# Dilated attention beside a state-space scan: the first weight columns loaded in another cut, and the order of every engine written anew

## The chip, the core and the metric

The kernel runs on one core of one Trainium2 chip. The time is device microseconds of one execution, from start to end. One execution was also recorded by the hardware profiler; its span, its rows and its chain of waits are what this document reads. Engine names are those of the profile: PE is TensorE's matmul side and PEld its weight loads, DVE is VectorE, ACT is ScalarE, POOL is GpSimd, SP is SyncE, whose sequencer here only issues DMAs.

## The reference, cut to what matters

Two independent layers work on inputs of their own, and their outputs stand side by side. A is attention with 16 heads of 28 channels over 2048 tokens, in which a token sees itself and seven earlier ones, two apart. B is a diagonal complex recurrence over the 2048 tokens with a projection in and out.

```python
S, D, H, Dh, W, dil = 2048, 448, 16, 28, 8, 2
# A
q, k, v = split_heads(x @ wqkv)                       # (H, S, Dh) each
logits = einsum("hsd,hswd->hsw", q, k[:, s - 2*w]) * Dh**-0.5   # -1e9 where s - 2w < 0
o = einsum("hsw,hswd->hsd", softmax(logits), v[:, s - 2*w])
a = merge_heads(o) @ wo
# B
Lam_bar = exp(exp(log_dt) * Lam)                      # 448 complex values
Bu = x @ (((Lam_bar - 1) / Lam)[:, None] * Bmat).T
for t in range(S): h = Lam_bar * h + Bu[t]; hs[t] = h
b = 2 * real(hs @ Cmat.T) + x * Dskip
out = concatenate([a, b], axis=-1)                    # (1, 2048, 896) bf16
```

## The kernel before

**The order is a string.** Each small function of the kernel is a step: it emits one group of instructions. `ORDER` names the steps one after the other, and the loop at the end calls them so. No scheduler moves anything afterwards, so every engine runs its own instructions in the order of the string, and an instruction that waits holds up everything behind it on its engine. In a name the digits are the arguments, `@` gives the PSUM banks that the step's matmuls write, and the last sign of an eviction (a copy out of PSUM) says which engine makes it: `.` is ACT, `=` is DVE; evictions without a sign that add something (`h`, `c`, `dn`) are DVE's.

**Attention's projections.** The 2048 tokens are two halves of 1024 (`u`), each of two blocks of 512 (`s`). The channels of q and k are cut into seven blocks `m`: 0, 2, 4 are 128 columns of q each, 1, 3, 5 the same of k, and 6 holds the last 64 of both, copied together by POOL (line 223). The contraction of 448 is three slices of 128 rows and one of 64; the slice of 64 rows is kept twice (partitions 0 to 63 and 64 to 127, `w_half`), so that the two token blocks run side by side on the two halves of the array. `QK u m 0` is the six matmuls of 128 rows, `QK u m 1` the two of 64, `QS m s` does one token block alone, `V_` is the same for v. `qk`, `qh`, `v` evict.

x must first be transposed. For tokens 0 to 1023 PE does it: `XI0`, `XI1`, `XI2` for tokens 0 to 511, `XH1`, `XA10`, `XA11` for tokens 512 to 1023, evicted by `xi`, `xh`, `xa`. For tokens 1024 to 2047 four DMA transposes do it (line 173).

**Logits and softmax.** `P u r w` (line 379) multiplies a block of q with four shifted views of k on DVE, 128 x 2048 elements into one of seven buffers; `E_ u r` sums such products over the channels of a head on PE. `lt`, `TD` (a DMA transpose), `sma`, `smb`, `smc` make the softmax of a half. `AL g` and `al` place its weights for four token tiles, `ad`, `sp` (four DMAs each) write them through DRAM into a banded matrix `PT`; `AX`, `ax`, `adx`, `spx` do the same for the seam between the halves. `AV B hg par` multiplies the band with v, `av` evicts into `oT`, `W_` applies `wo`, `w` evicts into one of six buffers `ya`, and `ow` stores.

**The recurrence.** `ty`, `tf`, `ts` make tables of sines (ACT and DVE), `BU` projects, `BR`, `z`, `UP`, `y` combine four tokens, `sa`, `sb`, `sd` scan on DVE, `DN`, `dn`, `H_`, `h` spread the states again, `ca` (two ACT instructions) and `cs` scale the output weights, `C` and `c` project and add, `oc` stores. The last product is cut in two (`CH`, `ch`, `oh`). `pg` is a row of 17 small DVE instructions, `rb` builds four rotation matrices.

**Loads.** All DMA of data is issued by SP but the first four, which ACT issues. Eight semaphores are used in turn, so that a DMA waits until the eighth before it has landed. `w_load(c, n, at)` loads `n` columns from `c` for 384 rows, one DMA for each offset in `at` (0 is q, D is k, 2D is v); `w_half(s, c, n, at)` loads the last 64 rows into half `s`.

Of the kernel before, what the change touches and what calls it, by code (L numbers as in the profile page):

```python
# [14 lines left out]
S, D, H, DH, W = 2048, 448, 16, 28, 8  # L15
# [14 lines left out]


ORDER = """
WU@0 XI0@0 xi00= xi01. XI1@1 XI2@2 xi10= xi11. PP@3 xi20. pcopy pa QS00@4 pb QS10@5 qk000. pd_ pc XH1@6 pe XA10@7
xh1. XA11@1 qk010. xa10= QK021@32 xa11. QK031@04 P000 ty0 QS01@6 pf QS11@5 P001 QK051@71 QK030 tf0 qk011. qk001. pg
ts00 QK050 qk031. ts10 ts20 QK020 qk051. P010 qk050. ty5 V_010@56 ty2 tf5 qk020. QK061@41 P011 V_001@73 ts05 V_011
V_000 v010. qk030. tf2 ts15 QK060 qk021= ts25 v000. P020 v001. QK040@50 qh001. rb2 v011. qh011. QK041 V_111@27 ty1
P021 V_101@36 V_110 qk040. qk041. tf1 ts02 E_00@50 P030 E_01 ts01 ts12 E_02 qh000. V_100 P031 qh010. v111. P040
QK130@41 ts22 ts11 v101. P041 v100. V_411@76 ts21 QK131 E_03 hc0 P050 ty6 E_04 ty4 V_410 qk131. tf6 qk130. QK100@31
P051 v411. ts06 v410. P060 QK110@46 ts16 BD v110. ts26 P061 QK101 ty3 QK151@72 QK111 qk100. E_05 rb0 qk101. E_06
qk110. QK150 tf4 lt00 P100 V_401@31 qk151. V_501@45 V_500 rb3 qk150. xt1 ts04 P101 lt01 QK120@27 ts14 qk111. tf3  # L40
v501. QK140@06 xt0 v500. P110 ts03 QK121 P111 QK141 qk120. QK161@54 V_400 qk140. xt3 P120 ts13 qk121. QK160 v400.
P121 qk141. v401. E_10@20 xt2 ts23 P130 E_11 ts24 V_510@73 qh101. P131 qh110. qh111. E_12 TD0 qh100. P140 E_13 hc1
V_511 P141 v511. v510. LC BU301@61 BU201@45 P150 BU300 sma0 BU200 OZ z30. XR BU400@37 z20. P151 smb0 BU000@64 P160
BR31 P161 BU001 ci1. BU401 E_14 z00. E_15 ci2= CD1 z40. E_16 rb1 z31. BR21 BR01 lt11 BU500@63 ci0= CD2 z21. smc0
z01. BU211@10 ci3. CD0 BU311@54 BU501 BU310 lt10 z50. CD3 BR32 BR41 BU210 z41. xd3 TD1 z32. BR51 xd2 BR22 AL0@2 z51.
BR33 z22. BU100@67 al0= z33. xd0 ca3 ad0 BU011@53 BU111@12 BU101 sma1 OP pm3 BU010 z10. pm0 wo UP3 AL1@6 cs3 smb1
BR11 xd1 BR02 BU110 z02. smc1 z11. BR03 al1. BR12 BU510@57 z03. ad1 z12. pm1 sp0 ca6 UP0 BR13 BU600@61 z13. y3. y0.
cs6 UP1 BR23 BU601 y1. z23. BU511 sa0 BU411@43 z60. BR52 pm4 ca1 BU410 sp1 sb0 BR61 z52. BR42 BU611@26 ca2 BU610 pm2
sd0 z61. AX@5 z42. BR53 BR62 AL2@1 ax= z53. z62. cs1 DN0@4 UP5 adx UP2 al2. DN1@5 BR43 dn0 BR63 y2. dn1 AL3@2 ad2
z63. sa2 H_10@1 y5. H_20@4 z43. H_11@0 al3. UP6 UP4 H_21@5 y6. H_00@7 ad3 y4. H_01@2 AV011@6 ca4 h21 spx AV010@3 h20  # L50
AV030@5 h01 av011. sp2 AV000@4 av010. cs2 AV020@6 av030. sb2 AV021@2 av000. AV001@3 av020. AV031@5 sd2 av001. W_00@4
sp3 av031. av021. W_20@6 ca5 h11 DN2@3 W_01@5 h00 DN3@2 dn2 w20. W_10@0 dn3 w01. sa4 ow20 W_11@7 ow01 W_21@3 w11.
w10. H_03@6 h10 H_02@2 w00. H_22@5 cs4 W_30@7 w21. ow00 sb4 H_23@0 ow21 H_13@1 w30. W_31@4 ow10 ca0 ow30 h13 AV100@3
ow11 h03 AV110@7 sd4 AV111@1 av110. AV131@6 av111. AV101@7 h02 av131. AV121@1 sa6 av101. AV130@6 av121. AV120@2 cs0
av130. DN5@7 av100. cs5 W_71@1 av120. dn5 W_61@6 w31. sb6 w71. h23 H_05@3 ow31 W_51@2 w61. ow71 ow61 W_41@7 w51= h05
H_15@4 ow51 H_25@1 W_50@0 h15 sd6 DN4@6 W_60@2 w50. w41. W_40@3 ow50 w60= ow41 DN6@4 C32@0 w40. ow60 dn6 dn4 ow40
h25 H_06@7 H_16@2 H_04@3 h06 H_12@4 H_14@6 h04 W_70@1 c32 H_24@7 C31@3 h22 oc32 w70= h12 C33@0 ow70 c31 h14 oc31
H_26@5 C30@1 c33 h26 oc33 h24 C02@4 c30 oc30 C20@3 c02 C00@6 c20 h16 oc20 CH0@0 c00 C01@5 oc00 C11@7 c01 ch0 oc01
C12@1 oh0 oc02 C13@4 C22@3 C03@2 c22 c12 oc22 c13 C21@6 oc12 c11 oc13 oc11 C10@5 c21 c03 oc21 CH1@0 oc03 c10 ch1
oc10 oh1  # L60
"""

# [1 line left out]
def kernel(  # L64
# [18 lines left out]
    ACT = nc.scalar  # L83
# [41 lines left out]
    def w_load(c, n, *at):  # L125

        for d in at:
            SP.dma_start(wq[:, 0:3, c + d:c + d + n], wq_r[:, :, c + d:c + d + n])  # L128

    def w_half(s, c, n, *at, eng=SP):  # L130

        o, i = (bass.AP(t.tensor, t.offset + c + at[0], [list(t.ap[0]), [D, len(at)], [1, n]])
                for t in (wq[64 * s:64 * s + 64, 3], A_wqkv[384:448]))
        eng.dma_start(o, i)
# [2 lines left out]
    for i, vec in enumerate((B_Lambda_re, B_Lambda_im, B_log_dt)):  # L137
        ACT.dma_start(raw[:, i], vec.rearrange("(g p) -> g p", p=64).unsqueeze(1).to_broadcast((G, 2, 64)))

    w_half(0, 0, 128, 0, D, eng=ACT)  # L140
    SP.dma_start(xnA[:, 0:2], xA_r[:, 0:2])
    SP.dma_start(xnA[:, 2:4], xA_r[:, 2:4])
    w_load(0, 128, 0, D)
    SP.dma_start(xnA[:, 4:8], xA_r[:, 4:8])
    w_half(1, 0, 256, 0, D)
    w_load(128, 128, 0, D)
    w_half(0, 128, 128, 0, D)
    w_load(256, 192, 0, D)
# [771 lines left out]
```

## Time and profile before

| | us |
|---|---|
| median of 3 runs (lowest, highest) | 133.71 (133.06, 136.21) |
| the profiled execution, whole | 132.89 |
| its span, first to last recorded work | 130.7 |
| PE busy, 1067 matmuls | 125.4 (96%) |
| DVE busy | 113.4 (87%) |
| ACT busy | 88.8 (68%) |
| first matmul on data (`XI0`) | 3.73 |
| first matmul of a projection (`QS00`) | 5.50 |
| last group of matmuls (`CH1`) starts | 126.95 |

The granted TensorE clock is full over the whole page. A time with a step's name is the start of that step's instructions in the trace; times count from the start of the span. Busy time of PE counts from a matmul's start to its modelled end, and neighbours overlap, so the text goes by the distance between starts.

### The profile page before, as it was taken

How to read it: one execution, taken by the hardware profiler on the slowest of the kernel's cores; microseconds unless marked ns; L12 is line 12 of the kernel's file. 1: busy time of each engine (PE TensorE's matmuls, PEld its weight loads, DVE VectorE, ACT ScalarE, POOL GpSimd, SP SyncE). 2: the span in 40 equal slices, each digit the busy share in tenths (PEclk: the TensorE clock that was granted, in tenths of full speed). 3: DMA queues.
4: the chain of work that ended last, by engine and by line, in shares of the span. 5: the costliest groups of instructions: out<-in, count | busy, mean ns of one | idle time of the engine just before them, and what ended most of it. 6: DMA issues, size and time to landing. Idle time of an engine off the chain costs nothing.

```text
span 130.7 us, 2869 instructions
## 1 busy us (share of the span) xinstructions
PE 125.4 (96%) x1067; PEld 62.2 (48%) x1067; DVE 113.4 (87%) x206; ACT 88.8 (68%) x185; POOL 19.8 (15%) x37
## 2 busy tenths in 40 slices
PE   6999999999999999999999999999899999999991
PEld 6543443434233334334454356854575555565550
DVE  5679999999999999999999899999997999752282
ACT  1779999999978996995979999997497300000000
POOL 6802000000000000200799920000000000000000
PEclk9999999999999999999999999999999999999999
DMA  3997989899999998999786999999412332213043
GB/s 116 238 207 174 326 230 167 197 197 258 139 259 210 212 200 187 310 303 209 209 200 222 185 169 293 255 179 185 141 54 70 105 105 94 87 55 103 0 146 118
DMA packets 47780, 23.24 MB, mean 178 GB/s; under 512 B 35639, under 2 KB 46711, under 8 KB 47767
## 3 DMA queue, kind: packets, MB, share of 16 engines
q1 hardware_dynamic: 47560, 23.03, 78.3%
q8 instruction: 8, 0.13, 0.4%
q10 hardware_dynamic: 207, 0.04, 0.2%
q14 instruction: 5, 0.04, 0.1%
HBM read 11.69 MB, written 6.37 MB: 138 GB/s over the span
## 4 chain that ended last, share of the span: by engine, by line
PE 80%; ACT 7%; DMA 6%; SPq 3%; issue 1%; DVE 0%; ACTq 0%
PE ps L244 38%; PE ps L807 15%; PE ps L547 6%; PE ps L534 5%; PE ps L391 5%; ACT ctmp L684 4%; DMA out_dram<-ya 3%; PE ps L722 3%; DMA wq<-in_A_wqkv_dram 3%; PE ps L788 3%; ACT Z L114 2%; SPq L128 2%; PE ps L348 1%; PE ps L827 1%; PE ps L395 1%
## 5 line engine op out<-in xcount | busy, mean ns | idle before, releaser
L379 DVE TENSOR_TENSOR pr<-qf,kf 128x2048 bf16<-128x2048 bf16 x24 | 28.7, 1236 | 0.1
L244 PE MATMUL ps<-xbuf,BT 128*128 128x512 bf16 (+1 forms) x112 | 23.6, 380 | 0.0
L244 PE MATMUL ps<-xT,wq 128*128 128x512 bf16 (+1 forms) x96 | 20.6, 380 | 0.1
L807 PE MATMUL ps<-Cw,Z 128*128 128x448 bf16 x105 | 20.5, 352 | 0.0
L114 ACT CAST Z<-ps 128x512 bf16<-128x512 f32 (+1 forms) x35 | 15.8, 520 | 3.0 <-PE ps L722 1.5
L813 DVE TENSOR_TENSOR xbuf<-ps,xnB 128x448 bf16<-128x448 f32 x15 | 9.0, 620 | 7.6 <-PE ps L807 7.5
L244 PEld LDWEIGHTS <-BT 128*128 128x128 bf16 (+1 forms) x112 | 8.9, 97 | 12.6 <-issue 3.5
L807 PEld LDWEIGHTS <-Z 128*128 128x128 bf16 x105 | 10.3, 98 | 9.4
L793 DVE TENSOR_TENSOR Z<-ps,Z 128x512 bf16<-128x512 f32 x21 | 13.7, 680 | 0.2 <-PE ps L788 0.2
L547 PE MATMUL ps<-wo,oT 128*128 128x448 bf16 x64 | 13.6, 353 | 0.0
L244 PEld LDWEIGHTS <-wq 128*128 128x128 bf16 (+1 forms) x96 | 7.8, 97 | 11.0 <-issue 2.3
L244 PE MATMUL ps<-wq,xT 128*128 128x448 bf16 (+1 forms) x64 | 13.0, 354 | 0.0
L877 POOL MEMSET PT<- 128x4320 f32 x3 | 11.0, 3698 | 7.2 <-DVE xnB L797 7.2
L114 ACT CAST ya<-ps 128x448 bf16<-128x448 f32 (+1 forms) x14 | 7.0, 566 | 5.5 <-PE ps L547 2.8
L684 ACT ACTIVATE ctmp<-Cw,c2t 64x448 f32<-64x448 bf16 x14 | 9.3, 667 | 0.3
L547 PEld LDWEIGHTS <-oT 128*128 128x128 bf16 x64 | 6.2, 98 | 5.7 <-ACT oT L114 0.2
L534 PE MATMUL ps<-PT,v_s 128*32 128x135 bf16 (+1 forms) x256 | 8.8, 298 | 0.0
L114 ACT CAST oT<-ps 128x512 bf16<-128x512 f32 x17 | 8.7, 620 | 0.1
L244 PEld LDWEIGHTS <-xT 128*128 128x128 bf16 (+1 forms) x64 | 4.8, 97 | 7.5 <-issue 4.1
L114 ACT CAST v_s<-ps 128x448 bf16<-128x448 f32 x16 | 8.2, 542 | 0.1
L534 PEld LDWEIGHTS <-v_s 128*32 128x32 bf16 x256 | 7.0, 110 | 0.7 <-ACT Z L114 0.4
L114 ACT CAST kf<-ps 128x512 bf16<-128x512 f32 x12 | 6.7, 582 | 0.7 <-PE ps L244 0.7
(150 smaller groups left out, 180.9 us busy)
## 6 DMA issues: line engine op xcount, KB each, us to landing
PT<-pd SPq DMA_DIRECT2D x16, 156.0 KB, 5.2
xnB<-in_B_x_dram SPq DMA_DIRECT2D x2, 896.0 KB
out_dram<-ya SPq DMA_DIRECT2D x16, 112.0 KB, 1.7
out_dram<-xbuf SPq DMA_DIRECT2D x15, 112.0 KB, 1.7
pd<-Ak SPq DMA_DIRECT2D x2, 640.0 KB, 3.5
xbuf<-in_A_x_dram SPq DMA_DIRECT2D x2, 448.0 KB
xnB<-in_B_x_dram SPq DMA_DIRECT2D x4, 224.0 KB, 5.4
xnB<-in_B_x_dram SPq DMA_DIRECT2D x4, 192.0 KB, 4.0
```

What stands on the lines that cost most here:

```text
L114: (ACT.copy if e == "A" else V.tensor_copy)(o, i)
L244: PE.matmul(o, l, r, start=(first and i == 0), stop=(not first and i == len(pairs) - 1 and not more[s]))
L379: V.tensor_tensor(t[:], q.unsqueeze(1).to_broadcast((128, 4, 512)), k4, ALU.mult)
L391: PE.matmul(acc[s][32 * i:32 * i + 32], E[:, f, ws, :], t[:, i, :], start=(f == 0 and ws == 0), stop=False)
L534: PE.matmul(p[32 * hh:32 * hh + 32, 128 * bl:128 * bl + n], v_s[:, t, 4 * hg + hh, :], PT[:, t % NS, (4 * hg + hh) // HS, (4 * hg + hh) % ...
L547: PE.matmul(p[:, 0:D], late["oT"][:, b // 4, hg, par, 128 * (b % 4):128 * (b % 4) + 128], late["wo"][:, hg, :], start=(hg == 0), stop=(hg ...
L684: ACT.activation(t[a:a + 64, 0:D], Cw[b:b + 64, g, :], ACTF.Copy, scale=c2t[a:a + 64, g:g + 1])
L722: PE.matmul(pp["z", g, j][:], rot(g, 0), late["Z"][:, g, j - 1, :], start=False, stop=True)
L793: V.tensor_tensor(zz, pp.pop(("h", j, g))[:], zz, ALU.add)
L807: PE.matmul(p[:, 0:D], z, Cw[:, g, :], start=(g == 0), stop=(g == G - 1))
L813: V.tensor_tensor(yo, pp.pop(("c", j, ct))[:, 0:D], xnB[:, ct, j, :], ALU.add)
L877: POOL.memset(late["PT"][:, 4 * i:4 * i + 4].rearrange("p t g n -> p (t g n)").bitcast(F32), 0.0)
```

## The change

The loads ahead of v are cut otherwise. Before, the first 128 columns of q and of k come ahead of tokens 512 to 1023 of x, in rows of 256 bytes; then the next 128 columns of both, then the last 192 of both. After, the first 256 columns of q alone come ahead of those tokens, in rows of 512 bytes, then all 448 columns of k in rows of 896 bytes, then the last 192 of q. SP issues nine weight DMAs in place of thirteen.

The first two products are therefore `QS00`, `QS20` (two blocks of q) in place of `QS00`, `QS10` (one of q, one of k), and the second token block follows with `QS01`, `QS21`. The whole string is another permutation: the steps are the same but for those, and ten evictions change between ACT and DVE (`xa11`, `qk051`, `ci1`, `av121` to DVE; `qk021`, `ci2`, `al0`, `ax`, `w60`, `w70` to ACT). Many PSUM banks change as well.

```diff
 ORDER = """
-WU@0 XI0@0 xi00= xi01. XI1@1 XI2@2 xi10= xi11. PP@3 xi20. pcopy pa QS00@4 pb QS10@5 qk000. pd_ pc XH1@6 pe XA10@7
-xh1. XA11@1 qk010. xa10= QK021@32 xa11. QK031@04 P000 ty0 QS01@6 pf QS11@5 P001 QK051@71 QK030 tf0 qk011. qk001. pg
-ts00 QK050 qk031. ts10 ts20 QK020 qk051. P010 qk050. ty5 V_010@56 ty2 tf5 qk020. QK061@41 P011 V_001@73 ts05 V_011
...
-z63. sa2 H_10@1 y5. H_20@4 z43. H_11@0 al3. UP6 UP4 H_21@5 y6. H_00@7 ad3 y4. H_01@2 AV011@6 ca4 h21 spx AV010@3 h20
-AV030@5 h01 av011. sp2 AV000@4 av010. cs2 AV020@6 av030. sb2 AV021@2 av000. AV001@3 av020. AV031@5 sd2 av001. W_00@4
-sp3 av031. av021. W_20@6 ca5 h11 DN2@3 W_01@5 h00 DN3@2 dn2 w20. W_10@0 dn3 w01. sa4 ow20 W_11@7 ow01 W_21@3 w11.
-w10. H_03@6 h10 H_02@2 w00. H_22@5 cs4 W_30@7 w21. ow00 sb4 H_23@0 ow21 H_13@1 w30. W_31@4 ow10 ca0 ow30 h13 AV100@3
-ow11 h03 AV110@7 sd4 AV111@1 av110. AV131@6 av111. AV101@7 h02 av131. AV121@1 sa6 av101. AV130@6 av121. AV120@2 cs0
...
+WU@0 XI0@0 xi00= xi01. XI1@1 XI2@2 xi10= xi11. PP@3 xi20. QS00@4 pcopy pa pb QS20@5 pd_ pc pe XH1@6 qk000. XA10@7
+ty5 XA11@0 xh1. xa10= ty0 QK051@13 xa11= pf QK011@24 tf5 QS01@6 QS21@7 tf0 qk020. QK010 pg qk021. ts05 ts00 V_010@05
+qk011. ts15 qk001. rb3 QK050 qk010. ts10 P000 ts25 QK040@74 qk050. ty2 qk051= ts20 V_001@62 P001 QK041 QK031@13
+qk041. V_011 V_000 ty1 tf2 v010. v011. rb0 QK030 v000. ts02 P010 QK060@40 qk031. ts12 tf1 ts22 V_100@56 qk030. P011
+ts01 qk040. V_101 P020 QK061 ty6 V_111@31 V_110 v001. v101. tf6 v100. QK131@72 ts11 P021 QK130 v110. v111. qh001.
...
+H_01@1 al3. H_20@4 h11 BR63 y5. H_10@2 ad3 h01 UP4 z63. H_00@5 adx H_21@6 y4. UP6 h10 ca4 AV010@7 sp2 sa2 AV020@1
+AV001@0 y6. av010. AV000@2 av020. h21 AV030@3 av000. AV011@7 sb2 spx av001. AV021@1 av030. AV031@6 av011. sd2 W_00@2
+sp3 av031. av021. W_30@0 ca1 h20 W_31@3 cs4 DN2@7 W_20@6 w31. cs1 w30. DN3@1 ow31 W_21@4 ca0 dn3 ow30 dn2 W_11@3 sa4
+w20. H_13@0 H_03@1 w21. W_01@7 ow20 w11. h00 H_02@6 w00. H_23@4 ow11 W_10@3 h13 ow00 sb4 ow21 H_22@5 H_12@2 w10.
+AV120@0 w01. ow10 h02 ca5 AV101@3 ow01 h22 AV111@7 sd4 AV100@6 av101. AV121@5 av120. av100. AV131@3 av111. av121=
+AV110@0 av131. h23 AV130@6 av110. sa6 DN5@7 DN4@5 av130. W_71@3 dn5 W_60@4 dn4 sb6 W_61@0 w60. cs0 W_41@6 w61. cs5
...
 """
...
-    w_half(0, 0, 128, 0, D, eng=ACT)
+    w_half(0, 0, 256, 0, eng=ACT)
     SP.dma_start(xnA[:, 0:2], xA_r[:, 0:2])
     SP.dma_start(xnA[:, 2:4], xA_r[:, 2:4])
-    w_load(0, 128, 0, D)
+    w_load(0, 256, 0)
     SP.dma_start(xnA[:, 4:8], xA_r[:, 4:8])
-    w_half(1, 0, 256, 0, D)
-    w_load(128, 128, 0, D)
-    w_half(0, 128, 128, 0, D)
-    w_load(256, 192, 0, D)
-    for s in range(2):
-        w_half(s, 256, 192, 0, D)
+    w_load(0, D, D)
+    w_half(1, 0, D, 0, D)
+    w_half(0, 0, D, D)
+    w_load(256, 192, 0)
+    w_half(0, 256, 192, 0)
     w_load(0, D, 2 * D)
     for s in range(2):
         w_half(s, 0, D, 2 * D)
```

More of the change, by code (lines that the diff above doesn't have):

```diff
@@ L32 @@
 ORDER = """
-WU@0 XI0@0 xi00= xi01. XI1@1 XI2@2 xi10= xi11. PP@3 xi20. pcopy pa QS00@4 pb QS10@5 qk000. pd_ pc XH1@6 pe XA10@7
-xh1. XA11@1 qk010. xa10= QK021@32 xa11. QK031@04 P000 ty0 QS01@6 pf QS11@5 P001 QK051@71 QK030 tf0 qk011. qk001. pg
-ts00 QK050 qk031. ts10 ts20 QK020 qk051. P010 qk050. ty5 V_010@56 ty2 tf5 qk020. QK061@41 P011 V_001@73 ts05 V_011
-V_000 v010. qk030. tf2 ts15 QK060 qk021= ts25 v000. P020 v001. QK040@50 qh001. rb2 v011. qh011. QK041 V_111@27 ty1
-P021 V_101@36 V_110 qk040. qk041. tf1 ts02 E_00@50 P030 E_01 ts01 ts12 E_02 qh000. V_100 P031 qh010. v111. P040
@@ L38 @@
[L38 to L47, printed above, removed]
@@ L48 @@
-cs6 UP1 BR23 BU601 y1. z23. BU511 sa0 BU411@43 z60. BR52 pm4 ca1 BU410 sp1 sb0 BR61 z52. BR42 BU611@26 ca2 BU610 pm2
-sd0 z61. AX@5 z42. BR53 BR62 AL2@1 ax= z53. z62. cs1 DN0@4 UP5 adx UP2 al2. DN1@5 BR43 dn0 BR63 y2. dn1 AL3@2 ad2
-z63. sa2 H_10@1 y5. H_20@4 z43. H_11@0 al3. UP6 UP4 H_21@5 y6. H_00@7 ad3 y4. H_01@2 AV011@6 ca4 h21 spx AV010@3 h20
-AV030@5 h01 av011. sp2 AV000@4 av010. cs2 AV020@6 av030. sb2 AV021@2 av000. AV001@3 av020. AV031@5 sd2 av001. W_00@4
-sp3 av031. av021. W_20@6 ca5 h11 DN2@3 W_01@5 h00 DN3@2 dn2 w20. W_10@0 dn3 w01. sa4 ow20 W_11@7 ow01 W_21@3 w11.
@@ L53 @@
-w10. H_03@6 h10 H_02@2 w00. H_22@5 cs4 W_30@7 w21. ow00 sb4 H_23@0 ow21 H_13@1 w30. W_31@4 ow10 ca0 ow30 h13 AV100@3
-ow11 h03 AV110@7 sd4 AV111@1 av110. AV131@6 av111. AV101@7 h02 av131. AV121@1 sa6 av101. AV130@6 av121. AV120@2 cs0
-av130. DN5@7 av100. cs5 W_71@1 av120. dn5 W_61@6 w31. sb6 w71. h23 H_05@3 ow31 W_51@2 w61. ow71 ow61 W_41@7 w51= h05
-H_15@4 ow51 H_25@1 W_50@0 h15 sd6 DN4@6 W_60@2 w50. w41. W_40@3 ow50 w60= ow41 DN6@4 C32@0 w40. ow60 dn6 dn4 ow40
-h25 H_06@7 H_16@2 H_04@3 h06 H_12@4 H_14@6 h04 W_70@1 c32 H_24@7 C31@3 h22 oc32 w70= h12 C33@0 ow70 c31 h14 oc31
@@ L58 @@
-H_26@5 C30@1 c33 h26 oc33 h24 C02@4 c30 oc30 C20@3 c02 C00@6 c20 h16 oc20 CH0@0 c00 C01@5 oc00 C11@7 c01 ch0 oc01
-C12@1 oh0 oc02 C13@4 C22@3 C03@2 c22 c12 oc22 c13 C21@6 oc12 c11 oc13 oc11 C10@5 c21 c03 oc21 CH1@0 oc03 c10 ch1
+WU@0 XI0@0 xi00= xi01. XI1@1 XI2@2 xi10= xi11. PP@3 xi20. QS00@4 pcopy pa pb QS20@5 pd_ pc pe XH1@6 qk000. XA10@7
+ty5 XA11@0 xh1. xa10= ty0 QK051@13 xa11= pf QK011@24 tf5 QS01@6 QS21@7 tf0 qk020. QK010 pg qk021. ts05 ts00 V_010@05
+qk011. ts15 qk001. rb3 QK050 qk010. ts10 P000 ts25 QK040@74 qk050. ty2 qk051= ts20 V_001@62 P001 QK041 QK031@13
@@ new lines @@
+qk041. V_011 V_000 ty1 tf2 v010. v011. rb0 QK030 v000. ts02 P010 QK060@40 qk031. ts12 tf1 ts22 V_100@56 qk030. P011
+ts01 qk040. V_101 P020 QK061 ty6 V_111@31 V_110 v001. v101. tf6 v100. QK131@72 ts11 P021 QK130 v110. v111. qh001.
+P030 E_00@65 qh000. E_01 qk130. P031 QK111@31 qh010. V_410@47 ts06 ts21 P040 qk131. E_02 qh011. E_03 P041 ts16 V_411
+hc0 QK101@20 ty4 QK110 P050 v411. BD ts26 tf4 QK100 ty3 qk111. P051 QK150@71 qk101. tf3 v410. qk110. QK120@04 P060
+ts03 qk100. ts04 P061 QK121 xt2 QK151 QK161@32 qk151. E_04 P100 qk150. E_05 qk120. E_06 P101 qk121. QK160 xt0 lt01
@@ new lines @@
+lt00 P110 V_511@17 ts13 E_10@04 ts14 qh101. P111 V_500@56 qh111. xt1 qh110. P120 V_510 qh100. ts24 P121 QK141@23
+v510. V_501 xt3 E_11 v501. P130 QK140 P131 V_400@16 TD0 qk140. v511. rb2 qk141. E_12 hc1 E_13 P140 v500. V_401 LC
+BU301@27 v401. BU201@35 BU200 P141 v400. ts23 sma0 BU300 OZ z20. XR BR21 BU400@61 z30. P150 smb0 BU000@32 ci0= P151
+BR31 z21. BU001 P160 BU401 E_14 z00. z31. E_15 CD0 ci1= z40. BU500@53 P161 ci3. CD1 ci2. BR01 smc0 BR41 BU210@76
+z41. CD2 z01. E_16 BU501 CD3 lt11 BU211 BU311@12 lt10 BR22 BU310 z50. TD1 xd0 z22. AL0@4 xd1 BR51 BR32 al0. BR23
@@ new lines @@
+AL1@0 z32. xd3 ad0 BU100@57 z51. al1. rb1 z23. ad1 BR33 ca3 BU011@41 OP pm3 BU111@30 sma1 BU101 BU010 pm0 wo z33.
+z10. xd2 UP2 smb1 UP3 BR02 BR11 BU110 cs3 z02. smc1 z11. BR03 y2. BR12 y3. BU600@54 pm1 z12. sp0 z03. ca6 UP0 BR13
+BU510@76 z13. y0. cs6 UP1 BU601 y1. BU611@23 BU511 z60. sa0 BU411@10 pm4 BR52 sp1 AL2@5 z52. BU410 ca2 sb0 BR42 pm2
+AX@7 z42. BR61 sd0 BR53 BU610 z61. al2. z53. ad2 BR43 cs2 UP5 DN1@1 z43. DN0@4 BR62 ax. dn1 AL3@5 z62. dn0 H_11@7
+H_01@1 al3. H_20@4 h11 BR63 y5. H_10@2 ad3 h01 UP4 z63. H_00@5 adx H_21@6 y4. UP6 h10 ca4 AV010@7 sp2 sa2 AV020@1
@@ L60 @@
+H_04@7 ow61 H_15@5 w41. W_40@4 h04 w71. ow41 h03 W_70@0 sd6 H_24@6 H_14@7 w70. W_50@3 h12 W_51@1 h15 w50. DN6@0 h24
+H_25@2 ow50 C32@3 dn6 h14 h25 H_06@5 H_16@6 H_26@0 C31@7 h16 c32 H_05@2 C12@6 h05 c31 C33@3 h06 oc31 h26 c12 C11@2
+c33 oc12 oc33 C20@7 c11 ow60 ow70 oc11 C22@5 c20 ow71 oc32 oc20 C03@0 c22 w40. oc22 C21@6 ow40 c03 w51= oc03 CH0@3
+ow51 C02@2 C13@7 c02 c21 oc02 ch0 C01@5 oc21 c13 oh0 oc13 C30@4 c01 oc01 C00@0 c30 oc30 C10@1 c00 oc00 CH1@2 c10 ch1
 oc10 oh1
```

## The prediction

> **What bounds the kernel now.** First the page: busy shares, the forty slices, and the chain that ended last.
>
> ```profile
> PE   6999999999999999999999999999899999999991
> DVE  5679999999999999999999899999997999752282
> ...
> PE 80%; ACT 7%; DMA 6%; SPq 3%; issue 1%; DVE 0%; ACTq 0%
> ```
>
> PE is full in every slice but the first and the last, and the chain runs through it. So a change that keeps all matmuls can gain only what PE waits. I then took the distances between the starts of PE's steps and split them. The shortest of each kind: a full `QK` or `BU` step 1.295, its 64-row part 0.216, a full `V_` 1.146 and its part 0.189, `QS` 0.853, `E_` 0.43, `AV` 0.465 (first half) and 0.49, `W_` 0.755, `BR` and `H_` 0.215, `C` 1.324. Times their counts: A's projections 32.2, `E_` 6.3, B up to the states 31.6, `AL` 1.8, `AV` 7.6, `W_` 12.1, `C` 21.2, warm-up and transposes 5.3, together **118.1**. Where the tile shape changes (128 rows to 64, 128 columns to 32, and back) a step takes 0.097 longer; the string has 51 such places, **4.9**. What single steps take beyond that is **2.9** of waits. With 1.06 ahead of the first matmul that makes 127.0; the last matmul group starts at 126.95 and runs 0.83, so 0.8 is left in pieces under 0.06 and in the last matmul's own end. The end needs 2.9 more (the last addition and its store), which neither version alters.
>
> The waits are at three places. The timeline of the first 22 us (columns: start, duration, instruction, idle time before it) shows the first:
>
> ```profile
> 8.02 0.25 PEld L319 LDWEIGHTS <-xbuf 128*64 128x64 bf16 x4 [0.49 <-DMA xbuf<-in_A_x_dram]
> 9.33 0.11 PEld L244 LDWEIGHTS <-wq 64*128 64x128 bf16 x4 [0.30 <-DMA wq<-in_A_wqkv_dram]
> 9.77 2.77 DVE L379 TENSOR_TENSOR pr<-qf,kf 128x2048 bf16<-128x2048 bf16 x2
> 10.55 1.69 SPq L157 DMA_DIRECT2D xbuf<-in_A_x_dram  x3
> 17.94 5.35 SPq L173 DMA_TRANSPOSE xT<-xbuf  x4
> ```
>
> `XH1` waits for tokens 512 to 1023 (0.29 over its own time), `QK021` for weight rows (0.19); with 0.28 of evictions ahead of them, 0.76 in front. In the middle there are four waits of 0.16 to 0.22, together 0.7. Then PE's and ACT's timelines at 92 to 99 us:
>
> ```profile
> 92.57 0.66 PE L534 MATMUL ps<-PT,v_s 128*32 128x135 bf16 x16
> 93.70 0.19 PE L528 MATMUL ps<-PT,v_s 128*32 128x7 bf16 x4 [0.47 <-ACT ya L114]
> ...
> 95.68 0.19 PE L528 MATMUL ps<-PT,v_s 128*32 128x7 bf16 x4 [0.25 <-ACT oT L114]
> ```
> ```profile
> 93.11 0.53 ACT L114 CAST ya<-ps 128x448 bf16<-128x448 f32 x1 [1.99 <-DMA out_dram<-ya]
> 93.67 1.35 ACT L684 ACTIVATE ctmp<-Cw,c2t 64x448 f32<-64x448 bf16 x2
> 95.05 3.52 ACT L114 CAST oT<-ps 128x512 bf16<-128x512 f32 x7
> ```
>
> The seventh eviction of `w` waits until the first store has left its buffer, `AV110` waits for that eviction's bank (0.68), `AV101` for an eviction that stands behind `ca0` (0.49); with `AV000` 0.28, that is 1.45.
>
> **The front, step by step.** The trace's packet records give a 256-byte packet 18 ns, 384 bytes 22, 512 bytes 27, 896 bytes 41 (medians), on 16 engines. Ahead of tokens 512 to 1023 stand 896 weight packets of 256 bytes, 896 x 18 / 16 = 1.01 us; after, 448 of 512 bytes, 448 x 27 / 16 = 0.76. SP issues these tokens one place earlier, at 2.38 in place of 2.91. So they come 0.25 to 0.53 earlier than 7.98: 7.45 to 7.73. `QS00` needs 0.22 more weight packets than now ((27 - 18) x 384 / 16), so they land at 5.25 in place of 5.03, and PE gets to it at 5.50: covered by 0.25. `QS20` has its weights with `QS00`'s and loses the 0.09 that `QS10` waited. PE is at `XH1` by 7.65; I take 7.7, a gain of 0.3.
>
> A rule of the Trainium skill, in "DMA: Bandwidth & Descriptors", section Specifications, bears on this: below 512 bytes a transfer is not at line rate, because the engine reads, modifies and writes. By it a 256-byte piece would cost what one of 512 costs, and `QS00`'s weights would come no later than now, where the rows give 0.22 later; with either it is covered.
>
> Then k: 384 packets of 896 bytes are 0.98, the two halves of its last rows 0.33 and 0.16, together 1.48 behind the tokens. Now 1.22 of packets stand there and take 1.31 (7.98 to 9.29), so 1.58: landing at 9.0 to 9.3. PE needs 1.12 from `XH1` to `QK051`, so 8.8; ACT ends the eviction it needs at about 8.9. `QK051` starts at 9.1 in place of 9.33, and `QS01` follows as it did. **Front: -0.25**, between 0 and -0.5.
>
> **Two steps behind it.** `QK131`, the first of tokens 1024 to 2047, now runs ahead of all `E_`: it stands 1.47 (`E_00` to `E_02`) earlier than 26.46, and the front's 0.25, so 24.7; its DMA transposes land at 25.05 now. Four SP issues fewer, at some 0.55 each, put their loads (10.55) and transposes (17.94) up to 2.2 earlier. Cover: 1.8; without it the wait is 0.35. I take 0.
>
> The first k block is now complete only behind `QS21` and `QK010`: 9.6 + 0.95 + 0.95 + 1.4 = 12.9, and `P000` after its eviction, third in ACT's row, at 15.2 in place of 9.77. DVE fills that time with work that stood later: `xa11` 0.42, two `tf` 1.6, `pg` 2.4, `rb3` 1.1, together 5.5 of 5.4. It is half a microsecond behind at most, and `E_16`, which waited on nothing but the last `P` (55.5), now comes at 58. Free, with 2 of cover.
>
> **The shape changes** are 52 in place of 51: +0.1. The Trainium skill, "TensorEngine Tiling (Array Packing)", section Key Properties, says that changing the tiling mode drains TensorE. The trace agrees (0.097 a place); that rule speaks against this order by one place, +0.1 by the row.
>
> **The middle.** None of the four waits belongs to the matmuls; each is a bank whose eviction was late, and banks and evictions are all dealt anew. Bounds: no wait, and twice the 0.7. I laid the steps of the new order end to end on each engine with the rows' durations and find two evictions of ACT that PE meets, ahead of `H_21` and `UP6`, some 0.2; another 0.1 I allow for lags that such a sum does not see. So 0.3 for 0.7: **-0.4**.
>
> **The attention's end.** `AL2` stands 4 us earlier against PE, and `ad2`, `ad3` ahead of `adx`; so the last band DMA, which lands at 92.41 now and just at `AV100`, lands near 91.2. But three waits take the place of those lost:
> - `W_00` now follows the eight `AV` directly. PE does them in 3.8. ACT first has `y6` behind `ca4` (1.35), and the fifth of its evictions, `av030`, ends 1.7 + 5 x 0.52 = 4.3 after the first `AV` starts. **+0.5.**
> - The seventh `w` (`w10`) still waits for the first store, `ow31`, issued at about 87.5; with the 4.4 that `ow20` takes now it ends at 91.9 to 92.2, and `w10` at 92.7. `AV101`, the second of its half (92.5), needs that bank: **+0.2**.
> - Behind it ACT has `w01`, `ca5` (1.35) and seven `av` of 0.52. `AV110`, `W_71` and `W_60` each run up to an eviction: **+0.7** in all.
>
> Together 1.4, against 1.45 now: **-0.05**, between -0.9 (the store is early, ACT keeps up) and +0.8.
>
> **Sum.** -0.25 (front), -0.4 (middle), -0.05 (attention's end), +0.1 (shapes): **-0.6**. The profiled execution took 132.89 (130.7 of span and 2.2 around it), so 132.3; the median of the runs stands 0.8 above it, and 133.71 - 0.6 is **133.1**.
>
> **Rivals.**
> 1. *k in whole rows comes late (slower).* `QK051` needs all 344 KB of k and both halves, and everything on PE stands behind it. For it: from 4.26, where tokens 256 to 511 have landed, to 7.98 the engines move 2.3 of packets (1.01 and 512 x 41 / 16) in 3.7, a pace of 0.62. At that pace 1.48 takes 2.4, k lands at 10.1, the front is +0.8 in place of -0.25 and the sum +0.45: 134.2. It decides from a landing after 9.7, where the front has eaten the rest. Against it: 1.31 for 1.22 in the very stretch. Chance 0.12.
> 2. *The attention's end is dealt worse.* `ow31` lands later than now, `AV101` and all evictions behind `ca5` slip: +0.8 to +1.5, 133.9 to 134.6, more if banks in the middle are caught too. Chance 0.15.
> 3. *The waits there go.* The store lands by 91.5, ACT keeps pace, -0.9: 132.2; if everything clears, 2.9 less 0.1 are gone, 130.9. Chance 0.2, of it 0.07 below 131.
> 4. *The wider pieces gain nothing.* x still lands at 7.98, as the slowest of 16 engines sets a landing: 133.35, inside the forecast's range. Chance 0.1.
>
> The forecast has 0.43. The range 131.3 to 135.2 takes in both ends of front and attention and leaves out 0.2. Within 2% of 133.71 (131.0 to 136.4), about what a measurement of this kernel can tell from no change, lie nearly all of these: faster 0.09, same 0.8, slower 0.11.
>
> **What would show it.** In the new profile: `XH1`'s weight load at 7.6 to 7.8, `QK051`'s at 9.0 to 9.3 with a short wait for wq; the three x loads issued near 8.3 and the transposes landed by 23; the first `P` at 15 with DVE unbroken to about 70; no wait of PE for PT; `W_00` waiting half a microsecond for ACT. A `QK051` after 9.6, a PE wait for xT near 25, or a DVE gap between 16 and 56 would make the prediction wrong.

## The result, and the profile after

The changed kernel takes **134.42 us** (median of 6 runs, 133.81 to 136.19), the kernel before 133.16 beside it (6 runs); the ratio is 1.010, with an interval of 1.007 to 1.013, over the runs of the fast state alone (two of the six after and one of the six before fell in a slower one, at 136.2). The forecast was 133.1, a gain of 0.6; it is a loss of 1.3. The profiled span is 132.3 in place of 130.7.

The slices and the chain on the page of the changed kernel, answering to the three lines of before:

```profile
PE   6688999999999999999999999999999999999990
DVE  5557989999999999999988899999999998753651
...
PE 72%; ACT 13%; DMA 7%; DVE 4%; issue 1%; SPq 1%
```

The second, third and fourth slice of PE are 6, 8 and 8 where before had three nines; the slice near 92 us that was an 8 is a 9. So time was lost ahead of 13 us, and some of it won back later. The timeline of the first 13 us says by what (PE's weight loads, which wait ahead of their matmuls, and SP's issues; start, duration, instruction, idle time before it):

```profile
6.52 0.33 PEld L347 LDWEIGHTS <-wq 128*128 128x128 bf16 x3 [0.96 <-DMA wq<-in_A_wqkv_dram]
...
9.35 0.25 PEld L318 LDWEIGHTS <-xbuf 128*64 128x64 bf16 x4 [0.90 <-DMA xbuf<-in_A_x_dram]
...
11.05 0.20 PEld L243 LDWEIGHTS <-wq 64*128 64x128 bf16 x4 [0.69 <-DMA wq<-in_A_wqkv_dram]
```
```profile
2.38 0.49 SPq L144 DMA_DIRECT2D xbuf<-in_A_x_dram  x1
...
10.49 1.47 SPq L156 DMA_DIRECT2D xbuf<-in_A_x_dram  x3
```

These are `QS00`, `XH1` and `QK051`, and each waits for a DMA. `QS00` starts at 6.53 and not at 5.50, `XH1` at 9.35 and not at 8.02, `QK051` at 11.05 where `QK021` started at 9.33. Over their own times the three waits are some 0.95, 0.67 and 0.58.

A DMA's landing is recorded in 16 parts, and PE may go on with the last. The trace's DMA records give for the three pieces (us; "12th" is the part with which three quarters are in):

```
piece                     issued  first  12th  last   before: last
q, 256 columns (L128)      1.84   4.38   5.27   6.48   5.03 (128 columns)
x, tokens 512..1023        2.38   6.20   7.20   9.30   7.98
k, 384 rows (L128)         2.91   7.24  8.93  10.47      -
k, 64 rows (L134)          3.57   7.82  9.31  10.77   8.24 (columns 0 to 255)
k, 64 rows (L134)          4.18   8.08  9.58  11.01   9.29 (columns 128 to 255)
```

Three quarters of q and of x come about when the prediction put them (5.25 and 7.45 to 7.73). The last parts come 1.2 and 1.6 later than it put them.

At the attention's end, PE's and ACT's timelines of the changed kernel:

```profile
97.80 0.19 PE L527 MATMUL ps<-PT,v_s 128*32 128x7 bf16 x4 [0.17 <-ACT oT L114]
```
```profile
95.79 1.34 ACT L683 ACTIVATE ctmp<-Cw,c2t 64x448 f32<-64x448 bf16 x2
97.16 3.03 ACT L114 CAST oT<-ps 128x512 bf16<-128x512 f32 x6
```

One wait that the profile names is left where there were two: ACT has the same long `ca` ahead of its `av`, but the waits of PE here sum to 1.0 where before had 1.45.

For all that follows, two readings per profile are enough: the start of `QS01`, the last step of the front, which both orders have behind the same work, and the way from there to the start of `CH1`, the last group of matmuls.

```
                QS00   XH1  first k step   QS01    CH1   CH1 - QS01
before          5.50   8.02      9.33      9.87  126.95    117.08
after           6.53   9.35     11.05     11.67  128.40    116.73
```

The front costs 1.80, everything behind it gains 0.35; together that is 1.45 of the 1.6 by which the span grew.

### The profile page after: what moved, and what is told of

It reads as the page before. It is cut to its first block, busy times and chain, and to the rows that moved or that the text cites. A ratio compares the mean times of both kernels' runs of the same rounds, so it can differ in the third digit from the quotient of the medians.

```text
span 132.3 us, 2851 instructions
## 1 busy us (share of the span) xinstructions
PE 124.9 (94%) x1058; PEld 62.1 (47%) x1067; DVE 112.3 (85%) x204; ACT 90.6 (68%) x187; POOL 19.9 (15%) x37
## 4 chain that ended last, share of the span: by engine, by line
PE 72%; ACT 13%; DMA 7%; DVE 4%; issue 1%; SPq 1%
PE ps L243 31%; PE ps L806 15%; PE ps L546 5%; DMA xbuf<-in_A_x_dram 5%; PE ps L533 4%; PE ps L721 4%; PE ps L390 3%; ACT ctmp L683 3%; DVE pr L378 3%; PE ps L787 3%; ACT ya L114 2%; ACT kf L114 2%; DMA out_dram<-ya 1%; PE ps L347 1%; ACT fr L642 1%
## 5 line engine op out<-in xcount | busy, mean ns | idle before, releaser
L378 DVE TENSOR_TENSOR pr<-qf,kf 128x2048 bf16<-128x2048 bf16 x24 | 28.1, 1219 | 0.6 <-ACT kf L114 0.6
L114 ACT CAST Z<-ps 128x512 bf16<-128x512 f32 (+1 forms) x35 | 16.3, 509 | 2.0 <-PE ps L243 0.7
L114 ACT CAST ya<-ps 128x448 bf16<-128x448 f32 (+1 forms) x16 | 8.0, 541 | 13.6 <-DMA out_dram<-ya 9.7
L114 ACT CAST qf<-ps 128x512 bf16<-128x512 f32 x12 | 7.0, 591 | 2.3 <-PE ps L243 1.6
L114 ACT CAST oT<-ps 128x512 bf16<-128x512 f32 x16 | 8.2, 628 | 0.0
```

The costliest lines, as they stand in the source:

```text
L114: (ACT.copy if e == "A" else V.tensor_copy)(o, i)
L378: V.tensor_tensor(t[:], q.unsqueeze(1).to_broadcast((128, 4, 512)), k4, ALU.mult)
```

## The experiments

Each ratio is against the kernel before, run beside it on the same chip.

**1. Both kernels once more, and two single undos.** Four kernels together: the changed one unaltered, the one before unaltered, and the changed one with one edit each:

```diff
 # q_two
-    w_load(0, 256, 0)
+    w_load(0, 128, 0)
+    w_load(128, 128, 0)
 # halves_first
-    w_load(0, D, D)
     w_half(1, 0, D, 0, D)
     w_half(0, 0, D, D)
+    w_load(0, D, D)
```

> The changed kernel once more, unaltered. Its profiled execution starts QS00 at 6.53, XH1 at 9.35, QK051 at 11.05 and QS01 at 11.67 (before: 5.50, 8.02, 9.33, 9.87), each behind a wait for a transfer whose last part lands up to 3 us after its first. Theory of the lasting straggler: the wider first piece of q leaves one or more of the 16 DMA engines behind in every execution; then QS01 starts at 11.2 to 12.1 again and the ratio stays at 1.008 to 1.012. Theory of chance: the profiled execution met one bad packet; then QS01 starts near 10 and what the 1.010 of the timed runs costs stands elsewhere, in the new order of the steps.

> The kernel before once more, for the spread of its front. Theory of the lasting straggler: QS00 at 5.5, XH1 at 7.9 to 8.2, QS01 at 9.7 to 10.1 as before, the last part of tokens 512 to 1023 within 2 us of its first. Theory of chance: the front moves by 0.5 or more from one execution to the next.

> The first 256 columns of q in two loads of 128 columns, 256-byte rows, in place of one with 512-byte rows; the order of the steps as after. Same bytes, 768 packets of 18 ns for 384 of 27: 0.22 more of packet time. Theory that the wide pieces leave an engine behind: QS00 back at 5.5 to 5.7, XH1 at 8.0 to 8.3, time 1.0 us shorter than after (ratio to before about 1.002). Theory that the volume ahead of the tokens and the order of the loads do it: XH1 stays at 9 or later, ratio 1.008 to 1.014.

> The two loads of the last 64 rows of q and k (0.33 and 0.16 of packets) stand ahead of the 344 KB of k in place of behind it; the order of the steps as after. QK051 and QK011 need only those. Theory that k in whole rows holds up PE (rival 1 of the prediction): QK051 starts about 0.5 earlier, at 10.5, right behind XA11 and its eviction, and the time falls by 0.4 to 0.6. Theory that the tokens' late landing is the limit: QK051 moves by less than 0.2, since the eviction of XH1 and XA10 ends at 10.4 to 11, and the time falls by under 0.2.

```
                ratio (interval)          QS00   XH1  QK051   QS01    CH1   CH1 - QS01
b_again         one run, 132.31           5.33   7.59     -    9.41  126.42    117.01
a_again         1.0077 (1.0044, 1.0110)   6.18   9.31  11.19  11.81  128.31    116.50
q_two           1.0030 (0.9990, 1.0069)   5.77   8.14  10.36  10.98  127.53    116.55
halves_first    1.0003 (0.9979, 1.0027)   6.35   8.49   9.61  10.24  126.72    116.48
```

Among these kernels with the new order, the changed one of the result with them, the last column stays within 0.25: all the rest of the difference between them arises before 12 us. The kernel before moved too: `QS01` is at 9.41, where its first profile has 9.87 and I had expected 9.7 to 10.1. So a difference of under half a microsecond between two single profiles decides nothing by itself. Of the 1.8 that the front lost, two narrow q pieces give back 0.7 to 0.8 and the 64-row key pieces ahead of the 384-row one 1.4 to 1.6, three times the 0.5 that the larger of my two expectations had. What waits at the first k step differs. PE's weight loads, of the kernel with two q pieces and of the one with the 64-row pieces first:

```profile
8.14 0.25 PEld L319 LDWEIGHTS <-xbuf 128*64 128x64 bf16 x4 [0.34 <-DMA xbuf<-in_A_x_dram]
...
10.35 0.20 PEld L244 LDWEIGHTS <-wq 64*128 64x128 bf16 x4 [1.20 <-DMA wq<-in_A_wqkv_dram]
```
```profile
6.34 0.33 PEld L347 LDWEIGHTS <-wq 128*128 128x128 bf16 x3 [0.90 <-DMA wq<-in_A_wqkv_dram]
...
9.61 0.11 PEld L243 LDWEIGHTS <-wq 64*128 64x128 bf16 x4
```

`QK051` multiplies only the last 64 rows (64x128 weights). With these behind the 384 rows it waits 1.20 for them (they landed at 10.06 and 10.31); with these first (8.71 and 8.90) it follows `XH1` and `XA` with no wait. The 384 rows themselves are first used by `QK010`, at 12.4 in that kernel. The wait that `QK051` had is 0.58 of the gain; the other 0.85 is there at `XH1` already (8.49 in place of 9.35), since x's last part came at 8.16 and not at 9.30. Why x came sooner with the 384-row piece farther behind it isn't shown.

Why is the wide q piece late? The packet records show rare packets that take many times the median. Three packets of 512 bytes in `a_again` took 1209, 985 and 813 ns, where the median is 27. Either rows of that width stall, or x, issued half a microsecond sooner, crowds the piece. The next kernels separate these. A third reading stays: `q_two` also lets `QS00` start on half of the bytes, whatever their width.

**2. Width or x's early issue; and both undos together.**

```diff
 # wide_b: the kernel before, with
-    w_load(0, 128, 0, D)
+    w_load(0, 256, 0)
+    w_load(0, 128, D)
...
-    w_load(128, 128, 0, D)
+    w_load(128, 128, D)
 # x_third: the changed kernel, with
     w_load(0, 256, 0)
+    w_half(1, 0, D, 0, D)
     SP.dma_start(xnA[:, 4:8], xA_r[:, 4:8])
     w_load(0, D, D)
-    w_half(1, 0, D, 0, D)
 # both: q_two and halves_first together
 # both_thirds: both, and
-    w_load(0, D, D)
+    w_load(0, 128, D)
+    w_load(128, 128, D)
+    w_load(256, 192, D)
```

> The kernel before, with its own order of all engines, and one edit: the first weight piece, 128 query and 128 key columns in 256-byte rows, becomes 256 query columns in 512-byte rows and then 128 key columns in 256-byte rows; the later piece of columns 128 to 255 loads keys alone. The number of loads ahead of x's tokens 512 to 1023 stays two, so x is issued at the same 2.9 us. If the width of the first packets makes them late: the first query step starts at 5.9 to 6.5 us (5.50 and 5.33 in the two profiles of before), the last of 16 parts of this piece lands at 5.8 to 6.4, and the time is 1.003 to 1.007 of before. If the piece came late in the changed kernel because x's load was issued 0.5 us sooner and took its share: the first query step at 5.4 to 5.7, by the larger piece alone (98 KB more, some 0.3 us at the pace of this stretch, ahead of the keys), and the ratio 1.000 to 1.003.

> The changed kernel with one load moved: the first 64-row key piece is issued between the wide query piece and x's tokens 512 to 1023, so that x is issued at some 2.9 us, as in the kernel before, and not at 2.4. The query piece stays one load of 512-byte rows. If the width of the first packets makes it late: its last part lands at 6.1 to 6.5 us as in the two profiles of the changed kernel (6.48 and 6.14), and the first query step starts at 6.2 to 6.6. If the early x made it late: last part at 5.2 to 5.7, the first query step at 5.3 to 5.8. Either way the key piece lands earlier than 10.8 (by some 2 us), and x later or as late as 9.3; the end follows the front: 116.5 us from QS01 on.

> The two edits of the last runs together: the first 256 query columns as two loads of 256-byte rows, and the two 64-row key pieces ahead of the 384-row key piece. Nothing is left out. If the loss is in the front alone, as the landings say, the two gains add up: TensorE's first query step near 5.7 us (as with the two loads), x's step for tokens 512 to 1023 near 8.1, the first key step near 9.3 to 9.5, the last step of the front (QS01) at 9.8 to 10.2, and 116.5 us from there to the last step, as with both edits alone: the last step starts at 126.3 to 126.7, against 126.4 and 126.95 of the two profiles of the kernel before. Time 0.995 to 0.999 of before. If the two gains are one and the same (what counts is when the 64-row key pieces land, and the query piece only moves a wait forward), the last step of the front stays at 10.2 and the ratio at 1.000.

> As the run with both edits, and the 384-row key piece in three loads (128, 128 and 192 columns) instead of one of whole 896-byte rows. If wide packets as such are what makes a piece late, the last part of the keys lands earlier than with the whole rows (9.49 and 9.80 us in the last runs), by some 0.3 us, and the front ends 0.1 to 0.3 earlier than in the run with both edits: ratio smaller by 0.001 to 0.002. If the stall belongs to the first transfers of the stream and not to the width, the three loads land as late as the one or later (two more issues of SP at some 0.5 us each, and three times the packets): same ratio as with both edits or up to 0.003 more.

```
                ratio (interval)          x issued  q last   QS00   XH1   QS01    CH1   CH1 - QS01
wide_b          1.0015 (0.9997, 1.0034)     2.91     6.20    6.25   8.86  10.61  127.51    116.90
x_third         1.0108 (1.0067, 1.0149)     2.98     6.53    6.57   9.52  11.69  128.19    116.50
both            0.9988 (0.9962, 1.0015)     2.91  6.11, 6.48  6.16   8.47  10.21  126.70    116.49
both_thirds     0.9978 (0.9950, 1.0006)     2.91  5.92, 6.27  5.97   8.15   9.90  126.39    116.49
```

PE's weight loads of `QS00` in `wide_b` and in `x_third`:

```profile
6.24 0.13 PEld L349 LDWEIGHTS <-wq 128*128 128x128 bf16 x2 [0.42 <-DMA wq<-in_A_wqkv_dram]
```
```profile
6.57 0.33 PEld L347 LDWEIGHTS <-wq 128*128 128x128 bf16 x3 [0.99 <-DMA wq<-in_A_wqkv_dram]
```

With x issued as late as before, the wide piece still lands at 6.20 and 6.53. So x's early issue is not what delays it; a wide first piece is late in the old order of loads too, and the kernel before then loses 0.7 to 1.2 in front. The time of `wide_b` (1.0015) is below the 1.003 to 1.007 that I had put on this, though, and inside the 1.000 to 1.003 of the other theory: the profiles speak for a late wide piece, the times do not. And the piece has twice the bytes of the narrow one that stood first. The two narrow ones of the kernel before are both in by 6.29 in one profile and 5.48 in the other. No run here loads the 256 columns in two pieces of wide rows, which would part the width from the cut. `x_third` shows one more thing: its first 64-row piece landed at 7.10, and nothing was won, since the second still stands behind the 384 rows (11.03, `QK051` at 11.07).

The two undos did not add up: `both` has `QS00` at 6.16 and the ratio of `halves_first`, within the intervals. In it the last of 16 parts of the first narrow piece landed at 6.11, when fifteen were in by 5.18. One 512-byte piece was left in these kernels, the 64 rows that ACT issues; in `both_thirds` one of its packets took 1092 ns. In `both` none of them took over 168 ns, so there it was something else; the longest ones of that stretch, up to 512 ns, were of x and of narrow q rows. `both_thirds` ends the front 0.3 sooner than `both`, as wide keys would have it, but its keys landed no sooner (10.11 and 10.09); what came sooner was x (8.11 and 8.42), which the edit leaves alone.

**3. All weight rows narrow, then x.**

```diff
 # all_narrow: both_thirds, and
-    w_half(0, 0, 256, 0, eng=ACT)
+    for c in (0, 128):
+        w_half(0, c, 128, 0, eng=ACT)
 # q_384: all_narrow, and
-    w_load(0, 128, 0)
-    w_load(128, 128, 0)
+    w_load(0, 192, 0)
+    w_load(192, 64, 0)
 # x_448: all_narrow, and
-    SP.dma_start(xnA[:, 4:8], xA_r[:, 4:8])
+    for d in (224, 0):
+        SP.dma_start(xnA[:, 4:8, d:d + 224], xA_r[:, 4:8, d:d + 224])
```

> As the run with both edits and the keys in three loads, and the 64-row query piece that ACT issues in two loads of 256-byte rows instead of one of 512-byte rows. So every weight row of the first query columns and of the 384-row key pieces up to column 255 is 256 bytes wide; 384 bytes for the last key columns, x's tokens as before. Nothing is left out. In the last two such runs the longest packets of the first microseconds stood in ACT's 512-byte piece (1092 ns at 4.05 us). If width makes packets stall: no packet over 300 ns in the query pieces (or one), the first query step at 5.3 to 5.7 us (5.97 with ACT's piece wide), x's step at 7.8 to 8.1, the end of the front at 9.5 to 9.9, and 0.994 to 0.998 of before. If the stalls come to whatever is first in the queues, or if ACT's second issue costs what the packets save: first query step at 5.9 to 6.2 and the ratio of both edits again, 0.998 to 0.999.

> As the run with all weight pieces narrow, but the two loads of the first 256 query columns are 192 and 64 columns wide (384 and 128 bytes) in place of 128 and 128; one size is changed. If the stalls begin at rows of 512 bytes: no packet over 300 ns among the 384 of 384 bytes (or one), the query pieces land within 0.15 us of those of the narrow run. If the stalls grow with width step by step: 2 to 4 such packets among the 384, and the last part of the query piece 0.2 to 0.5 later.

> As the run with all weight pieces narrow, and x's tokens 512 to 1023 in two loads of 448-byte rows (columns 224 to 447 first) in place of one of 896-byte rows. Nothing is left out. If rows of 512 bytes and more are what stalls (packets over 300 ns: 14.5 per 1000 of 512 bytes, 7.1 of 896, 1.2 of 256 over ten profiles): x's last part lands at 7.2 to 7.7 us and not near 8.1, x's step begins at 7.4 to 7.9 and the ratio is 0.001 to 0.003 below that of the run with narrow weights alone. If narrow rows cost per packet (the Trainium skill, DMA: Bandwidth & Descriptors, has transfers of 512 bytes and more at line rate and smaller ones below it): twice the packets and one more issue of SP put x's landing 0.2 to 0.5 later, at 8.3 to 8.6, the keys behind it too, and the ratio 0.001 to 0.004 above.

```
                ratio (interval)          q last       x last   QS00   XH1   QS01    CH1   CH1 - QS01
all_narrow      0.9995 (0.9972, 1.0018)   5.22, 5.92    8.54    5.84   8.64  10.38  127.16    116.78
q_384           one run, 133.03           5.34, 5.63    8.56    5.73   8.61  10.35  127.14    116.79
x_448           0.9980 (0.9957, 1.0002)   5.50, 5.87    8.08    5.54   7.68   9.53  126.87    117.34
```

With no 512-byte row left, the 384 rows of q's 256 columns are in by 5.6 to 5.9, in four profiles of four (the fourth follows below); the five profiles with one wide piece have 6.1 to 6.5. This, too, is less than it seems: where q is in two narrow pieces but ACT's is wide, the second landed at 6.65 (`q_two`), 6.48 and 6.27, as late as the one wide piece. In `all_narrow` the packets behave as the first theory says: between 3.2 and 6.5 us none of the 896 of 256 bytes took over 300 ns. `q_384` is between its two expectations: two of its 384 packets of 384 bytes took over 400 ns (the number that I had put on stalls that grow with width), but the piece landed 0.3 sooner and not later. But `all_narrow` gained nothing, and its ratio misses what I expected. x's last part came at 8.54; of the 582 packets of 896 bytes in the same stretch ten took over 300 ns, the longest 1033. The stalls are now in the next wide piece, x. That x is what PE waits for is plain in `q_384`, not in `all_narrow`. PE's steps `QS00`, `QS20` and `XH1`, first in `all_narrow`, then in `q_384`:

```profile
5.84 1.46 PE L351 MATMUL ps<-xT,wq 128*128 128x512 bf16 x3
...
7.57 0.82 PE L351 MATMUL ps<-xT,wq 128*128 128x512 bf16 x3
...
8.64 0.41 PE L322 MATMUL ps<-ident,xbuf 128*64 128x128 bf16 x4
```
```profile
5.73 0.82 PE L351 MATMUL ps<-xT,wq 128*128 128x512 bf16 x3
...
6.87 0.82 PE L351 MATMUL ps<-xT,wq 128*128 128x512 bf16 x3
...
8.61 0.41 PE L322 MATMUL ps<-ident,xbuf 128*64 128x128 bf16 x4 [0.59 <-DMA xbuf<-in_A_x_dram]
```

In `all_narrow` the three matmuls of `QS00` stand 0.4 apart and not 0.22, and `XH1` follows `QS20` directly. The trace's record of the full TensorE clock begins at 7.31 there (7.24 in `wide_b`, 4.1 to 5.5 in the other twelve), although the page shows it full from the start. PE is late there by itself, and `QS00` says nothing of q; in `q_384`, too, it follows the transposes without a wait.

`x_448` cuts x's rows, and its last part lands at 8.08, though SP issues its second half 0.4 later than `all_narrow` the one load (4.01 and 3.63). That is sooner than the 8.54 of `all_narrow` by 0.46, but later than the 7.2 to 7.7 that I had put on it; three kernels with x whole, issued at 2.4 to 2.9, have 8.1 to 8.2 (`q_two`, `both_thirds`, `halves_first`). The front ends at 9.53, 0.85 before that of `all_narrow`. Some 0.4 of that is not width at all. `XH1` transposes columns 384 to 447 alone, which lie in the half that is loaded first, in by 6.70, so only `XA10` behind it waits. The other 0.46 is a difference of two landings, each of one profile. PE's weight loads of `XH1` and `XA10`:

```profile
7.68 0.25 PEld L323 LDWEIGHTS <-xbuf 128*64 128x64 bf16 x4 [0.23 <-issue]
8.13 0.67 PEld L309 LDWEIGHTS <-xbuf 128*128 128x128 bf16 x12 [0.20 <-DMA xbuf<-in_A_x_dram]
```

The Trainium skill, "DMA: Bandwidth & Descriptors", section Specifications, has smaller transfers than 512 bytes below line rate; by it x would have come later, which it did not. The trace agrees in part. Over the first 11 us of all 14 profiles the bytes per ns by the median packet rise evenly, 14 at 256 bytes, 18 at 448, 19 at 512, 22 at 896, with no step at 512. In the mean the order turns: a packet of 448 bytes takes 27.0 ns, one of 512 takes 38.0, so per byte the wide one is dearer.

And then 0.5 to 0.8 of it is lost again at one place. PE's and SP's timelines of `x_448`:

```profile
25.71 1.58 PE L248 MATMUL ps<-xT,wq 64*128 64x512 bf16 x7 [1.02 <-ACT v_s L114]
```
```profile
10.37 1.69 SPq L161 DMA_DIRECT2D xbuf<-in_A_x_dram  x3
...
17.30 6.08 SPq L177 DMA_TRANSPOSE xT<-xbuf  x4
```

This is `QK131`, the first of tokens 1024 to 2047. The profile names an ACT eviction; the last DMA transpose landed at 25.62, and that is what it needed. Three key loads and two of x instead of one each had put SP's later issues back: in `both` SP issued the three x loads of tokens 1024 to 2047 at 8.98, and the last transpose landed at 22.86.

**4. Narrow rows only where something waits.** The keys' 384 rows are not needed before 11 us, so they can be one load.

```diff
 # x_448_k1: x_448, and
-    w_load(0, 128, D)
-    w_load(128, 128, D)
-    w_load(256, 192, D)
+    w_load(0, D, D)
```

> As the run with x's tokens 512 to 1023 in two loads of 448-byte rows, but the 384-row key piece is one load again instead of three, behind the 64-row pieces. In that run the front ended 0.4 us before the kernel before's first profile (QS01 at 9.53) and the gain was then lost at one place: tokens 1536 to 2047 were transposed by 25.62 us, their first step (QK131) waited for that until 25.71, 1.09 us, since the loads behind took two more issues of SP each. Nothing is left out. If the narrow rows of x bring the front forward and only SP's issues gave it back: QS01 again at 9.4 to 9.7, the keys' one load lands by 10.2 (first used at 11.7), the last transpose lands at 23.7 to 24.7, QK131 starts at 24.5 to 24.9, CH1 at 125.9 to 126.4, and 0.992 to 0.996 of before. If the early x of that run was luck of one profile (its timed runs gave 0.998): QS01 at 9.9 to 10.3 and 0.997 to 1.000.

It takes **132.52** (12 runs, 132.34 to 133.12) beside 133.13 for the kernel before: **0.9953, interval 0.9921 to 0.9985**. PE's weight loads, PE's step `QK131` and SP's issues in its profile:

```profile
5.69 0.33 PEld L350 LDWEIGHTS <-wq 128*128 128x128 bf16 x3
...
7.94 0.25 PEld L321 LDWEIGHTS <-xbuf 128*64 128x64 bf16 x4 [0.23 <-issue]
...
9.06 0.12 PEld L246 LDWEIGHTS <-wq 64*128 64x128 bf16 x4
```
```profile
24.77 1.57 PE L246 MATMUL ps<-xT,wq 64*128 64x512 bf16 x7
```
```profile
9.30 1.69 SPq L159 DMA_DIRECT2D xbuf<-in_A_x_dram  x3
```

From `QS00` on no weight load of the front waits for a DMA, SP's issue is 1.07 earlier than in `x_448`, the last transpose lands at 23.59, and `QK131` runs unhindered. `QS01` is at 9.69, the keys landed at 9.69, `CH1` starts at 126.51, 0.1 later than the range I gave. So the new order with these loads is faster than the kernel before by 0.6, by the timed runs. It is the only one of the kernels tried whose interval lies wholly below 1. The profiles place a part of it: `QS01` stands between the two profiles of before (9.87 and 9.41), and the way from there is 116.82 where those have 117.08 and 117.01, 0.2 to 0.3 less. `CH1` lies between theirs as well (126.95 and 126.42), so where the rest comes from isn't shown, nor whether the loads alone would give it in the order of before, which no run has.

## Why the prediction was wrong, point by point

**The front, -0.25: wrong, +1.80, and this is the whole miss.** The failing step is the landing times. `QS00`'s weights at 5.25, "covered by 0.25": they came at 6.48. x at 7.45 to 7.73: 9.30. k at 9.0 to 9.3: 11.01 for the part that counts. I had worked each out as a number of packets times the median of its size over 16 engines. That is the pace of a usual packet, and it fits three quarters of the parts; PE waits for the last of 16. That this one is late by the few packets that stall is inferred: their lengths (up to 1472 ns) are of the size of the lag, but the records do not say which of the 16 engines a packet was on. I took wide rows as the cheaper ones because their median per byte is lower; in the kernel before, the wide rows at that place were x's, and the gap between its 12th part and its last (7.21 and 7.98) was there to be read.

**The keys, 1.48 of packets behind the tokens.** I treated the three key pieces as one landing. `QK051` needs only the 64-row ones, and the change had put them behind the others. The order of two loads was worth 1.4 of the front by `halves_first`, 0.58 by this wait and 0.85 by x's sooner landing, more than the cut of q (0.7 by `q_two`), and neither the sum nor a rival had it: rival 1 says that `QK051` needs all 344 KB of k.

**Rival 1 (k late, 134.2)** gave the right sign and one of the three steps: it put k at 10.1 and the front at +0.8, from a pace of 0.62 that was in the trace. It had 0.12. That its time is so near is luck in part: it has +0.45 where +1.26 was measured, and starts from 133.71, the median of three runs, where six gave 133.16. Its reason was bytes, and the runs point to another; but its evidence, 2.3 of packets that took 3.7, was the sign of the stalls, and I had set it aside for 1.31 against 1.22 behind x, a stretch after the stalls.

**The middle, -0.4: wrong, about +0.1.** Four waits went as foreseen, and four others came: `QK101` 0.29, `QK150` 0.25, `UP5` 0.18, `AL3` 0.07, together 0.8 for 0.7. Of my two evictions ahead of `H_21` and `UP6` neither shows.

**The attention's end, -0.05: better, -0.45.** `W_00` and `AV101` were to cost 0.5 and 0.2; they cost 0.07 and 0.06. What else is there: `AV121` 0.41, `H_23` 0.22, `H_02` 0.19 and two more of 0.06 to 0.07, 1.0 for 1.45. **The shape changes** are 52, as said. So middle, end and shapes together came to -0.26 by these waits and -0.35 by the starts of `QS01` and `CH1`, against -0.35 forecast: right in sum, but by luck: two errors cancel.

**The two steps behind the front: right, without effect.** The transposes landed at 24.03 (I had asked for 23), `QK131` came at 26.77 and did not wait. The three loads were issued at 10.49 and not at 8.3: each waits until the DMA eight places before it has landed, and those were the late ones. The first `P` ran at 17.29 in place of the 15.2 expected, as late as the front, and PE waited for nothing of DVE's there.

**Rivals 2 and 3** (the end worse, the waits there gone) did not decide; 3 was half right. **Rival 4**, x still at 7.98, was on the right road, the slowest of 16, and stopped short of a loss.

## What to carry to other kernels

Where an engine waits for a whole transfer, read the last of its parts and not the median packet: compare the time when three quarters are in with the last one (0.8 apart before, 1.2 and 2.1 after the change), and try narrower rows, or a cut that lets the first step start on its part, where the gap is what an engine waits for. Order the pieces by who needs them first, down to the 64 rows of a matmul, before thinking of their width. And each load that is cut in two costs its queue an issue of half a microsecond, which comes back at the next DMA that is late: cut only what is waited for.

## What the runs showed of the hardware

The share of packets that stall jumps between rows of 448 and of 512 bytes. Between 1.5 and 11 us of all 14 profiles:

```
bytes   packets  median ns  mean ns  over 100 ns  over 300 ns  longest ns
256      12800       18       20.3      0.5%        0.15%         491
384       9920       22       28.6      0.6%        0.10%         891
448       2048       25       27.0      0.8%        0.15%         831
512       2752       27       38.0      2.9%        1.45%        1472
896      22006       41       50.7      2.7%        0.93%        1033
```

This is not a matter of place in the stream alone: between 3.2 and 6.5 us of all 14 profiles, 13 of 7579 packets of 256 bytes took over 300 ns, 3 of 1805 of 448 (x's tokens in the last two kernels), 40 of 2514 of 512 and 52 of 7189 of 896. For 384 bytes the one profile with them at that place (2 of 384) leaves it open. What stalls them isn't shown. Nor is why x's last part came at 9.3 to 9.5 in three profiles, those with a wide q piece and the 384 key rows right behind x, and at 8.1 to 8.7 wherever one of the two was changed. No run has the changed order of engines with exactly the loads of before, since its second step needs the columns that these bring last.
